# RWKV-style attention with a feed-forward chain: its small products on column halves, the first bonuses summed on TensorE, k and v without padding, and a new order of block 0

## The chip, the cores and the metric

The kernel runs on one NeuronCore of a Trainium2 chip. Its time is the device time of one execution in microseconds (us), as a median of three runs. A core has TensorE (PE, matrix products into PSUM), VectorE (DVE), ScalarE (ACT), GpSimd (POOL, which can't read PSUM) and SyncE (SP), which here only issues DMAs. ACT issues some DMAs at the start too. Each engine works through its own instructions in order; semaphores join them.

## The reference

A linear attention with decay, over 4 batches, 8 heads, 768 steps and 48 channels a head, and behind it two feed-forward parts on the 3072 tokens:

```python
for t in range(S):                       # state: (B, H, 48, 48)
    cur = u * k[t] (outer) v[t]
    y[t] = r[t] @ (state + cur)
    state = w * state + k[t] (outer) v[t]
x = y as (B*S, 384)
h = x @ w_in                             # 384 -> 2048
x = (max(h, 0) + alpha * min(h, 0)) @ w_out
h = ((x @ w1) * (x @ w2)) @ w3           # 384 -> 1024 -> 1024
return h @ w_out2                        # 1024 -> 384
```

The weights come as 64-bit floats.

## The kernel before

**Tiling.** The 768 steps are cut in 6 blocks of 128. In each block the 8 heads are taken as 4 pairs; a pair in a block, with all 4 batches, is a unit (24 units, n = 0 to 23; the pairs are taken in the order 3, 0, 1, 2, so units 0 to 3 are pairs 3, 0, 1, 2 of block 0). The two heads of a pair lie in partitions 0 to 47 and 64 to 111 where channels are on partitions.

**A unit's steps** have short names that the order of the work is written in. `ld` loads r and k with channels on partitions (`rk`) and r, k, v with steps on partitions (`nat`; in the loads of units 0 to 3 these parts are called r, k, a, b, v, with the unit's number). `rs` and `ks` (L178, L184) scale r and k by powers of w (`pw`), `S` (L239) multiplies them to 128x128 scores, `q` (L194) and `red` (L206) make the bonus u·r·k of each step as a sum over channels, `am` (L213) puts it on a diagonal, `fill` (L250) copies the scores in beside it under a mask. `kk` (L228) scales k for the state, `U` (L255) makes the state's update as a product of it with v, `car` (L270) adds it to the state. `Y` (L285) makes the output: the state product (state with `rs`, in blocks 1 to 5 only) and, into the same PSUM tile, the value products (v with `am`). The value products write each head on its own column half of TensorE's array (outputs from PSUM partition 0 or 64); the update and the state product use up to 112 columns at once. `ph` and `pl` (L333, L338) split y into a high and a low part for the feed-forward part, and `mv` (L326, L306) moves the rows of pair 3 by DMA into free partitions of the others' tile `x`: unit 0's into chunk 2, unit 1's into chunk 0, unit 2's into chunk 1.

**The feed-forward part** takes three products for each (high by high, low by high, high by low). In a block it has 16 features f: `P` (L475) is the first product (9 matmuls over the three chunks of `x`), `r` and `s` the activation (ACT, then DVE at L493), `hl` splits the result (ACT, then POOL), `D` (L512) the second product (9 matmuls into `acc`).

**The weights of the first part** are made in block 0 from 64-bit words: `is` or `issue` loads a raw tile (SP), `cA` (L117, ACT) widens it, `cd` (L122, three DVE instructions, with the PSUM bank `uy` as scratch) assembles the 32-bit value, `cB` (ACT) rounds it to the high part, `cl` (L138) makes the low part, on DVE for the features in WIV and WOV and on POOL for the others. There are 32 such tiles: w_in of feature 0, then by turns w_in of f+1 and w_out of f (`cdi11` would be w_in of feature 11).

**Order.** Everything is scheduled by hand. Block 0 and the preparation of block 1 run by the list STARTUP (L49): each word is a step, issued to its engines in that order. LOADS (L64) is the order of the first loads; words with a star go over ACT's queue, the others over SP's. The lists in L46 and L47 say which engine takes which unit's step: RV and KV the units whose `rs` and `ks` are on DVE (else POOL), AMA those whose `am` is on ACT (else DVE), CARA those of block 0 whose `car` is on ACT. Blocks 1 to 4 repeat the pattern MIDDLE (L37), block 5 has LAST; in blocks 1 to 4 a unit's `U` and `Y` follow each other on TensorE.

**Ahead of TensorE's first work** it multiplies zeros (`warm`, L740): WARM = 6 products of 128x512.

Of the kernel before, what the change touches and what calls it, by code (L numbers as in the profile page):

```python
# [17 lines left out]
P = 128  # L18
C = 128
# [9 lines left out]
R = 64 + D  # L29
VW = 2 * 64  # L30
ZERO = 64
WARM = 6
LEAD = 1
# [11 lines left out]
ORDER = (3, 0, 1, 2)  # L45
RV, KV, AMA, CARA = (1, 2), (0, 1, 2, 4, 5, 6), (0, 1, 2, 3, 5, 7), (2, 3, 6, 7)  # L46
WIV, WOV = (3,), (0, 4, 5, 7, 10, 11, 14, 15)  # L47
PIN = 16
STARTUP = """  # L49
ld4 q0 rs0 pw0 ks0 S0 red0 ks1 rs1 am0 S1 fill0 ks2 rs2 q1 kk0 U0 q2 red1 am1 Y0 red2 fill1 S2 q3 ph0 cA issue1  # L50
red3 Y1 rs3 issue1 am2 pl0 mv0 ks3 car0 cd ph1 am3 S3 fill2 Y2 ld5 fill3 ph2 cB kk1 pl1 pl2 mv1 Y3 cA U1 cd ks4
mv2 cB cA cA q4 red4 cl issue1 car1 kk3 cl cd cB cd ph3 cl issue1 issue1 issue1 rs4 cB pl3 U3 mv3 P0 cA am4 q5
r0 P1 is cA cl cd s0 r1 kk4 cd S4 kk2 hl0 P2 cB cl U2 fill4 car3 cB cl cA r2 s1 hl1 cA Y4 cd U4 cB car2 P3
issue1 cd cA cl cB s2 r3 D0 cd ks5 cA rs5 issue1 ld6 cl is cB s3 P4 ph4 is is cl D1 hl3 is hl2 cA cd issue1 cB
r4 is is red5 car4 pl4 cd s4 am5 cB cl cA hl4 cl D2 cA cd mv4 P5 S5 is cB kk5 cl cd r5 is s5 cB cA cl cA cd
fill5 hl5 ld7 cB P6 r6 cl cA cd cB D3 s6 rs6 cl cd U5 hl6 ks6 P7 r7 cB s7 cA cl cA cd cd Y5 cB is kk6 cl D4 is
ph5 cA car5 cB q6 cl hl7 P8 D5 r8 red6 is cd P9 is s8 S6 cB pl5 cA cd cl hl8 r9 cB is cl D6 q7 is am6 cA cd cA
s9 cB is cl hl9 cd P10 is cB cl cA r10 fill6 cA cd cB ks7 s10 cA cl cd hl10 D7 cd rs7 P11 is r11 s11 cB cl Y6
kk7 ph6 cB hl11 U6 cl cA mv5 cA D8 cd cB is is cd P12 r12 cB s12 D9 cl cA cl pl6 car6 cA cd hl12 cB P13 cd r13
cl D10 cd cl s13 cA S7 ld8 cd cB cl mv6 hl13 is cA red7 cB P14 cl q8 am7 cd fill7 r14 cA cA cB cd is D11 P15 ks8  # L60
cA U7 s14 cd Y7 kk8 rs8 cB r15 cd is ph7 D12 cl is D13 s15 cB cl cA car7 hl15 cl is red8 pl7 hl14 mv7 is cB am8
ld9
"""
LOADS = """  # L64
b1 r0* a0 k3 keep* a1* a2 b0 v0 k1 r1* v3 v2 brief* k0* a3* k2* r2 b2 v1 r3 b3
"""
# [4 lines left out]
def tile_kernel(ctx: ExitStack, tc: tile.TileContext, a: dict, out: bass.AP):  # L71
# [18 lines left out]

    w_sb = const.tile([R, NHP], F32, name="w_sb")
    keep = const.tile([P, P + DM + M1], F32, name="keep")
# [5 lines left out]
    w128 = const.tile([R, NHP, 1], F32, name="w128")  # L98
    w2 = const.tile([P, NHP, R], F32, name="w2")
    state = const.tile([R, NHP, B, R], F32, name="state")  # L100
# [48 lines left out]
    def load(n, now=True):  # L149
        i, hp = UNITS[n]  # L150
        cuts = [0, B * 2 * D, B * (2 * D + R), B * (2 * D + R + VW)]
        src = [a["rkT"][i, hp, :, m] for m in range(2)]
        src += [a["nat"][i, hp, :, lo:hi] for lo, hi in zip(cuts, cuts[1:])]
        if n in (2, 3):
            w = "wi" if n == 2 else "wo"
            t = [spare(f"{w}{11 + m}", list(x.shape), f"in{m}") for m, x in enumerate(src)]
        else:
            rk = ld.tile([R, 2, B, C], F32, tag="rk", name="rk")
            nat = ld.tile([P, cuts[-1]], F32, tag="nat", name="nat")
            t = [rk[:, 0], rk[:, 1]] + [nat[:, lo:hi] for lo, hi in zip(cuts, cuts[1:])]  # L160
            if now:
                nc.sync.dma_start(out=rk, in_=a["rkT"][i, hp])
                nc.sync.dma_start(out=nat, in_=a["nat"][i, hp])
        if not now:
            fetch.update({f"{x}{n}": (t[m], src[m]) for m, x in enumerate("rkabv")})
        un[n] = dict(
            rk=t[0:2],
            r=t[2].rearrange("p (b j d) -> p b j d", b=B, j=2),
            k=t[3].rearrange("p (b d) -> p b d", b=B),
            v=t[4].rearrange("p (b d) -> p b d", b=B),  # L170
        )
# [22 lines left out]
    def prep_q(n):  # L194
        i, hp = UNITS[n]
        t = un[n]
        q1 = work(n, [P, B, 2, D], "q1", "wi8")
        t["q1"] = q1
        nc.gpsimd.tensor_tensor(
            out=q1, in0=t["r"], in1=bc(u_sb[:, hp], B).rearrange("p b (j d) -> p b j d", j=2), op=ALU.mult  # L200
        )
        k = t["k"]
        heads = bass.AP(k.tensor, k.offset, [list(k.ap[0]), [R, B], [64, 2], [1, D]])
        nc.gpsimd.tensor_tensor(out=q1, in0=q1, in1=heads, op=ALU.mult)

# [22 lines left out]
    def prep_k2(n):  # L228
        i, hp = UNITS[n]
        t = un[n]  # L230
        if i < NB - 1:
            if 0 < n < NHP:
                k2 = spare("wi9" if n == 2 else "wo8", [P, B, R], "k2")
            else:
                k2 = wk.tile([P, B, R], F32, tag="k2", name="k2")
            nc.gpsimd.tensor_tensor(out=k2, in0=t["k"], in1=bc(w2[:, hp], B), op=ALU.mult)
# [18 lines left out]
    def update(n):  # L255
# [4 lines left out]
        pool, tag = (ps_a, f"acc{2 * (n % 2)}") if n < NHP else (ps_s, "s")  # L260
        pu = pool.tile([R, B, 2, D], F32, tag=tag, name="pu")
        for b in range(B):
            nc.tensor.matmul(
                out=pu[:, b],
                lhsT=t["k2"][:, b], rhs=t["v"][:, b].rearrange("p (j d) -> p j d", j=2)[:, :, 0:D],
                start=True, stop=True,
            )
        t["pu"] = pu

    def carry(n):  # L270
# [4 lines left out]
        for j in range(2):  # L275
            s = state[64 * j:64 * j + D, hp, :, 64 * j:64 * j + D]
            if i == 0:
                (nc.scalar.copy if n in CARA else nc.vector.tensor_copy)(out=s, in_=pu[64 * j:64 * j + D, :, j])
                continue
            nc.vector.scalar_tensor_tensor(  # L280
                out=s, in0=s, scalar=w128[64 * j:64 * j + D, hp],
                in1=pu[64 * j:64 * j + D, :, j], op0=ALU.mult, op1=ALU.add,
            )

    def out_y(n):  # L285
        i, hp = UNITS[n]
# [412 lines left out]
    def transposes(_):  # L699
        pw2 = ps_u.tile([P, NHP, P], F32, tag="uy", name="pw2")  # L700
        for hp in range(NHP):
            nc.tensor.transpose(
                out=pw2[:, hp, 0:R], in_=up[:, hp, ZERO - 1:ZERO - 1 + C], identity=ident[0:R, 0:R]
            )
        nc.scalar.copy(out=w2, in_=pw2[:, :, 0:R])

    with tc.manual_schedule():
        todo += first_weights()
        nc.sync.dma_start(out=w_sb, in_=a["w"])
        junk = wk.tile([P, N], F32, tag="am", name="junk", bufs=2)  # L710
        nc.vector.memset(junk, 0.0)
# [134 lines left out]
def layout(x):  # L846
# [20 lines left out]
    rn = toks(r).reshape(NB, NHP, C, B * 2 * D)  # L867
    kn = np.zeros((NB, NHP, C, B, 2, 64), k.dtype)
    kn[..., :D] = toks(k)
    kn = kn.reshape(NB, NHP, C, B, P)[..., :R].reshape(NB, NHP, C, B * R)  # L870
    vn = np.zeros((NB, NHP, C, B, VW), v.dtype)
    vn[..., 0:D] = toks(v)[..., 0, :]
    vn[..., 64:R] = toks(v)[..., 1, :]
    o["nat"] = np.ascontiguousarray(np.concatenate([rn, kn, vn.reshape(NB, NHP, C, B * VW)], axis=3))
# [57 lines left out]
```

## Time and profile before

| | us |
|---|---|
| median of 3 runs | 861.36 |
| lowest and highest | 859.84, 861.59 |
| the profiled execution | 858.42 |
| its span, first to last instruction | 856.6 |
| TensorE busy in it | 831.0 |
| POOL, DVE, ACT busy | 388.2, 387.0, 347.3 |

TensorE's records of 32-bit products come in two per product; "x16" stands for 8 products. Busy times of matmuls overlap, so the time that one takes in a sequence is read from its start to the next one's start. In a row of a timeline stand the start and the duration in us, engine, line, operation, output<-inputs, shape and count, and in brackets the idle time before it with what ended it. Rows of the page and the trace stand below, in groups.

### The profile page before, as it was taken

Reading aid. Unit: us, or ns where it says so; the run is one execution under the profiler, and the core shown is the slowest. Engines: PE = TensorE matmul, PEld = TensorE weight load, DVE = VectorE, ACT = ScalarE, POOL = GpSimd, SP = SyncE. Lnnn points to the kernel's source line nnn. Section 1 sums busy time; section 2 is a strip of 40 time slices with the busy share of each in tenths; the row PEclk is TensorE's granted clock in tenths of the full one; section 3 lists DMA queues with packets and bytes.
Section 4 is the critical chain, followed back from the end, with each engine's and each line's share of the span. In section 5 each row is a group of like instructions: output and inputs, shape, how many; then the busy total and the mean of one; then the engine's idle time right before and its main releaser. Section 6 shows DMA issues by size and latency. Waiting matters only on the chain.

```text
span 856.6 us, 11700 instructions
## 1 busy us (share of the span) xinstructions
PE 831.0 (97%) x4320; PEld 686.5 (80%) x4320; DVE 387.0 (45%) x611; ACT 347.3 (41%) x689; POOL 388.2 (45%) x327
## 2 busy tenths in 40 slices
PE   7599999999999999999999999999999999999997
PEld 4487788888888888888888888888888888888885
DVE  6889997987697777763332211111110101010100
ACT  3576675555555554544334442221222222222121
POOL 5676875666577658664432252121141322323211
PEclk8899999999999999999999999999999999999999
DMA  9656565776777776733223550432100202020001
GB/s 280 200 191 195 150 198 176 233 241 214 227 226 194 207 214 203 209 113 102 83 78 115 197 186 19 135 135 99 44 31 0 75 1 74 0 74 1 1 37 42
DMA packets 45445, 111.37 MB, mean 130 GB/s; under 512 B 5249, under 2 KB 12546, under 8 KB 45378
## 3 DMA queue, kind: packets, MB, share of 16 engines
q1 hardware_dynamic: 44290, 108.81, 40.7%
q10 hardware_dynamic: 1088, 1.71, 0.7%
q8 instruction: 36, 0.59, 0.3%
q14 instruction: 31, 0.25, 0.1%
HBM read 80.88 MB, written 27.26 MB: 126 GB/s over the span
## 4 chain that ended last, share of the span: by engine, by line
PE 89%; DVE 5%; DMA 2%; issue 2%; ACT 1%; SPq 0%; POOL 0%; DVEq 0%; ACTq 0%
PE acc L114 11%; PE acc L113 11%; PE acc L115 11%; PE ph L113 8%; PE ph L114 7%; PE ph L115 7%; PE pb L114 4%; PE pa L114 4%; PE pa L115 4%; PE pb L115 4%; PE pb L113 4%; PE pa L113 4%; PE sc L246 2%; PE py L299 2%; PE py L292 2%
## 5 line engine op out<-in xcount | busy, mean ns | idle before, releaser
L110 POOL TENSOR_TENSOR gl<-g,gh 128x512 fp32r<-128x512 f32 x96 | 125.4, 1307 | 173.2 <-ACT gh L109 168.8
L110 POOL TENSOR_TENSOR gl<-p,gh 128x512 fp32r<-128x512 f32 x48 | 62.1, 1293 | 238.2 <-ACT gh L109 238.2
L770 DVE TENSOR_TENSOR p<-p,pb 128x512 f32<-128x512 f32 x48 | 33.0, 688 | 249.9 <-PE pb L115 249.9
L113 PE MATMUL ph<-x,wi 128*128 128x512 f32 x288 | 117.2, 407 | 3.9 <-DMA x<-e 3.4
L493 DVE SCALAR_TENSOR_TENSOR g<-g,keep,p 128x512 f32<-128x512 f32 x80 | 71.8, 897 | 105.2 <-ACT p L488 95.1
L114 PE MATMUL ph<-x,wi 128*128 128x512 f32 x288 | 113.9, 395 | 2.7 <-POOL wi L139 2.7
L115 PE MATMUL ph<-x,wi 128*128 128x512 f32 x288 | 113.2, 393 | 0.0
L113 PE MATMUL acc<-gh,wo 128*128 128x512 f32 x288 | 112.5, 391 | 0.0
L115 PE MATMUL acc<-gl,wo 128*128 128x512 f32 x288 | 112.3, 390 | 0.0
L114 PE MATMUL acc<-gh,wo 128*128 128x512 f32 x288 | 112.1, 389 | 0.0
L765 ACT COPY p<-pa 128x512 f32<-128x512 f32 x48 | 28.2, 587 | 200.6 <-PE pa L115 200.6
L487 ACT ACTIVATE g<-ph 128x512 f32<-128x512 f32 x96 | 57.2, 596 | 88.4 <-PE ph L115 83.6
L109 ACT CAST gh<-g 128x512 fp32r<-128x512 f32 x96 | 59.3, 619 | 67.2 <-DVE g L493 66.5
L113 PEld LDWEIGHTS ph<-x,wi 128*128 128x128 f32 x288 | 54.6, 189 | 19.6 <-ACT wi L136 4.3
L114 PEld LDWEIGHTS ph<-x,wi 128*128 128x128 f32 x288 | 54.6, 190 | 15.1 <-POOL wi L139 4.8
L115 PEld LDWEIGHTS ph<-x,wi 128*128 128x128 f32 x288 | 54.5, 189 | 11.5
L115 PEld LDWEIGHTS acc<-gl,wo 128*128 128x128 f32 x288 | 54.1, 188 | 11.6 <-POOL gl L110 0.4
L113 PEld LDWEIGHTS acc<-gh,wo 128*128 128x128 f32 x288 | 54.1, 188 | 11.6 <-issue 0.3
L114 PEld LDWEIGHTS acc<-gh,wo 128*128 128x128 f32 x288 | 54.1, 188 | 11.1
L115 PE MATMUL acc<-gl,m 128*128 128x512 f32 x144 | 56.2, 390 | 0.0
L114 PE MATMUL acc<-gh,m 128*128 128x512 f32 x144 | 56.1, 390 | 0.0
L113 PE MATMUL pa<-x,w 128*128 128x512 f32 x144 | 56.0, 389 | 0.0
(106 smaller groups left out, 1617.0 us busy)
## 6 DMA issues: line engine op xcount, KB each, us to landing
nat<-in_nat SPq DMA_DIRECT2D x20, 672.0 KB, 6.7
raw<-in_wA SPq DMA_DIRECT2D x32, 384.0 KB, 3.6
s<-raw SPq DMA_DIRECT2D x32, 384.0 KB, 3.5
rk<-in_rkT SPq DMA_DIRECT2D x20, 448.0 KB, 6.4
raw<-in_wB SPq DMA_DIRECT2D x16, 384.0 KB, 4.4
raw<-in_w3T SPq DMA_DIRECT2D x16, 384.0 KB, 4.6
w<-s SPq DMA_DIRECT2D x16, 384.0 KB, 3.1
x2d<-o SPq DMA_DIRECT2D x18, 256.0 KB, 2.4
```

The source lines that it names most:

```text
L109: nc.scalar.copy(out=dst_h, in_=src)
L110: (lo or nc.gpsimd).tensor_tensor(out=dst_l, in0=src, in1=dst_h.bitcast(F32), op=ALU.subtract)
L113: nc.tensor.matmul(out=o, lhsT=wh, rhs=xh, start=first, stop=False)
L114: nc.tensor.matmul(out=o, lhsT=wl, rhs=xh, start=False, stop=False)
L115: nc.tensor.matmul(out=o, lhsT=wh, rhs=xl, start=False, stop=last)
L246: nc.tensor.matmul(out=sc[j][:, b], lhsT=t["ks"][o:o + D, b], rhs=t["rs"][o:o + D, b], start=True, stop=True)
L292: nc.tensor.matmul(out=py[:, b], lhsT=state[:, hp, b], rhs=t["rs"][:, b], start=b == 0, stop=False, skip_group_check=True,)
L299: nc.tensor.matmul(out=py[o:e, b], lhsT=t["v"][:, b, o:e], rhs=t["am"][:, B * j + b], start=i == 0 and b == 0, stop=True, skip_group_check ...
L487: nc.scalar.activation(out=g, in_=ph, func=ACTF.Relu, scale=-1.0)
L493: nc.vector.scalar_tensor_tensor(out=g, in0=g, scalar=alpha[:, f:f + 1], in1=p, op0=ALU.mult, op1=ALU.add)
L765: nc.scalar.copy(out=g, in_=pa)
L770: nc.vector.tensor_tensor(out=g, in0=g, in1=pb, op=ALU.mult)
```

## The change

- k and v lie in DRAM and in the tiles without padding: 384 columns each, where k had 448 and v 512.
- Update (L255): two products per batch, one a head, each with 48 weight columns and 48 streamed columns, on the column half of its head; before, one product of 112 weight columns and 96 streamed ones. k2 has 384 columns in place of 448.
- State product (L285): two products per batch, of 64 and 48 weight columns, on the two column halves; before, one of 112.
- Value products: as before, with v's new offsets.
- Bonus of units 0 to 2 (QPE): `q` is one DVE instruction on the tiles with channels on partitions (u times k times r), `red` four products on TensorE with a two-column tile of ones (`heads`), into PSUM bank `uy`, and a copy on ACT. The `a` loads of these units are left out, and w comes together with u (`wu`).
- RV, KV, AMA, CARA, WIV and WOV have new members. `ks` of units 1, 2, 4, 5, 6 goes from DVE to POOL, `rs` of unit 0 from POOL to DVE, `am` of unit 2 from ACT to DVE, `car` of unit 1 from DVE to ACT; five low halves of weights are on DVE in place of nine.
- STARTUP and LOADS have new orders. ACT issues five of the first loads, not eight.
- Ahead of TensorE's first work stand 14 products of zeros of 128x256.

```diff
-WARM = 6
+WARM = 14
-RV, KV, AMA, CARA = (1, 2), (0, 1, 2, 4, 5, 6), (0, 1, 2, 3, 5, 7), (2, 3, 6, 7)
-WIV, WOV = (3,), (0, 4, 5, 7, 10, 11, 14, 15)
+RV, KV, AMA, CARA = (0, 1, 2), (0,), (0, 1, 3, 5, 7), (1, 2, 3, 5)
+WIV, WOV = (3, 5, 15), (11, 14)
+MVA = 0
+QPE = (0, 1, 2)
 STARTUP = """
-ld4 q0 rs0 pw0 ks0 S0 red0 ks1 rs1 am0 S1 fill0 ks2 rs2 q1 kk0 U0 q2 red1 am1 Y0 red2 fill1 S2 q3 ph0 cA issue1
-red3 Y1 rs3 issue1 am2 pl0 mv0 ks3 car0 cd ph1 am3 S3 fill2 Y2 ld5 fill3 ph2 cB kk1 pl1 pl2 mv1 Y3 cA U1 cd ks4
-mv2 cB cA cA q4 red4 cl issue1 car1 kk3 cl cd cB cd ph3 cl issue1 issue1 issue1 rs4 cB pl3 U3 mv3 P0 cA am4 q5
...
+ks1 ks3 pw0 ks0 rs0 ld4 S0 kk0 q0 red0 rs1 am0 rs2 U0 q1 S1 red1 q2 am1 fill0 Y0 q3 fill1 Y1 rs3 S3 car0 cA ph0
+cA red3 pl0 cd ks2 issue1 red2 S2 kk1 am2 fill2 mv0 rs4 q4 ph1 am3 Y2 U1 ph2 fill3 cB red4 ks4 cd pl1 cA cd pl2
+issue1 ld5 mv1 cB issue1 mv2 issue1 cA Y3 car1 cl cB kk3 cl cd ph3 pl3 S4 mv3 U3 cB P0 cl cA q5 r0 cd cl is cB
+cA am4 P1 r1 kk2 cl is s0 cd hl0 s1 car3 cB cA is U2 fill4 cl P2 kk4 hl1 is cA r2 cd cB rs5 U4 issue1 cl P3 is
+Y4 car2 cd cA is ld6 cB r3 s2 issue1 cd issue1 cl D0 s3 cA cB P4 ph4 issue1 cl is D1 issue1 hl3 hl2 cA cd car4
+cB kk5 r4 red5 ks5 D2 am5 cd cl s4 cB cA pl4 cl hl4 cd P5 cA cB D3 is is cl S5 ld7 cd P6 r5 cA s5 cB cl hl5 cA
...
 LOADS = """
-b1 r0* a0 k3 keep* a1* a2 b0 v0 k1 r1* v3 v2 brief* k0* a3* k2* r2 b2 v1 r3 b3
+brief k3 a1 b3* b1 k2 a0 r0 r1 keep b0* v0* a3 v2 a2 r2 k1* r3 b2 v3 v1 k0*
...
     def prep_q(n):
+        if n in QPE:
+            t["q1"] = q1 = work(n, [R, B, C], "q1", "wi8")
+            nc.vector.scalar_tensor_tensor(
+                out=q1, in0=t["rk"][1], scalar=wu[:, 1, hp:hp + 1], in1=t["rk"][0][:, :, ::-1],
+                op0=ALU.mult, op1=ALU.mult,
+            )
+            return
...
     def bonus(n):
+        if n in QPE:
+            pq = ps_u.tile([P, B * 2], F32, tag="uy", name="pq")
+            for b in range(B):
+                nc.tensor.matmul(
+                    out=pq.rearrange("p (j b) -> p b j", j=2)[:, b], lhsT=t["q1"][:, b], rhs=heads, start=True, stop=True
+                )
+            nc.scalar.copy(out=t["q"], in_=pq)
+            return
...
     def update(n):
-        pu = pool.tile([R, B, 2, D], F32, tag=tag, name="pu")
+        pu = pool.tile([R, B, D], F32, tag=tag, name="pu")
         for b in range(B):
-            nc.tensor.matmul(
-                out=pu[:, b],
-                lhsT=t["k2"][:, b], rhs=t["v"][:, b].rearrange("p (j d) -> p j d", j=2)[:, :, 0:D],
-                start=True, stop=True,
-            )
+            for j in range(2):
+                h = slice(D * j, D * j + D)
+                nc.tensor.matmul(
+                    out=pu[64 * j:64 * j + D, b], lhsT=t["k2"][:, b, h], rhs=t["v"][:, b, h], start=True, stop=True
+                )
...
     def out_y(n):
+        sides = [(64 * j, min(64 * j + 64, R)) for j in range(2)]
         if i > 0:
             for b in range(B):
-                nc.tensor.matmul(
-                    out=py[:, b], lhsT=state[:, hp, b], rhs=t["rs"][:, b], start=b == 0, stop=False,
-                    skip_group_check=True,
-                )
+                for o, e in sides:
+                    nc.tensor.matmul(
+                        out=py[o:e, b], lhsT=state[:, hp, b, o:e], rhs=t["rs"][:, b],
+                        start=b == 0, stop=False, skip_group_check=True,
+                    )
...
-        warm = ps_h.tile([P, N], F32, tag="h", name="warm")
-        for _ in range(WARM):
-            nc.tensor.matmul(out=warm, lhsT=junk[:, 0:P], rhs=junk, start=True, stop=True)
+        def busy(k):
+            held = any(("U", n) in fin and ("car", n) not in fin for n in (0, 2))
+            idle = ps_a.tile([P, 2 * P], F32, tag="acc2" if held else "acc0", name="idle")
+            for _ in range(k):
+                nc.tensor.matmul(out=idle, lhsT=zeros[:, 0:P], rhs=zeros, start=True, stop=True)
...
+        busy(WARM)
```

## Rows read from the trace of the kernel before

**Rows 1.** The page's busy time of each engine (us, share of span, instructions).
```profile
PE 831.0 (97%) x4320; PEld 686.5 (80%) x4320; DVE 387.0 (45%) x611; ACT 347.3 (41%) x689; POOL 388.2 (45%) x327
```

**Rows 2.** Who waited for whom, TensorE, 40 to 125 us: total, times, longest.
```profile
PE ph L113 <- DMA x<-e: 3.4, 1, 3.4
PE ph L114 <- POOL wi L139: 2.7, 4, 1.0
PE ph L113 <- ACT wi L136: 0.6, 1, 0.6
```

**Rows 3.** Busy us in the window: PE, PEld, DVE, ACT, POOL, then clock, DMA.
```profile
80.00:100.00 20.00, 18.35 (x90) 14.00 (x90) 18.59 (x34) 12.50 (x25) 15.48 (x15) 1.00 0.61 192
```

**Rows 4.** Timeline of the start: start, duration, engine, line, what, idle before.
```profile
3.39 0.34 ACTq L719 DMA_DIRECT2D brief<-in_brief  x1
...
11.03 0.81 DVE L188 TENSOR_TENSOR ks<-rk,pw 112x512 f32<-112x512 f32 x1 [3.31 <-ACT pw L732]
...
14.39 1.48 DVE L182 TENSOR_TENSOR rs<-rk,pw 112x512 f32<-112x512 f32 x1
...
19.67 1.87 PE L299 MATMUL py<-am,nat 128*64 128x128 f32 x16
...
35.49 2.55 SPq L308 DMA_DIRECT2D x<-e  x4
...
41.13 0.77 PE L113 MATMUL ph<-x,wi 128*128 128x512 f32 x1 [3.36 <-DMA x<-e]
...
42.08 1.69 DVE L220 TENSOR_TENSOR am<-keep,q 128x1024 f32<-128x1024 f32 x1
```

**Rows 5.** Timeline of TensorE: update, state, value products of a unit in block 1.
```profile
196.54 0.93 PE L263 MATMUL pu<-nat,k 128*112 128x96 f32 x8
197.31 1.05 PE L292 MATMUL py<-rs,state 112*112 112x128 f32 x8
198.29 1.09 PE L299 MATMUL py<-am,nat 128*64 128x128 f32 x16
199.31 0.50 PE L113 MATMUL ph<-x,wi 128*128 128x512 f32 x1
199.65 0.39 PE L114 MATMUL ph<-x,wi 128*128 128x512 f32 x1
```

**Rows 6.** Chain of waits and timeline, TensorE in block 0: records at both clocks, S4.
```profile
42.33 0.43 PE ph L115
...
45.79 0.23 PE ph L115
...
47.33 1.16 PE L246 MATMUL sc<-rs,ks 48*128 48x128 f32 x16
48.42 0.50 PE L113 MATMUL ph<-x,wi 128*128 128x512 f32 x1
```

**Rows 7.** Groups by form, weight loads, 180 to 380 us: busy us, mean ns.
```profile
L263 PEld LDWEIGHTS pu<-nat,k 128*112 128x112 f32 x72 | 8.4, 177 | 0.8
...
L299 PEld LDWEIGHTS py<-am,nat 128*48 128x48 f32 x72 | 7.4, 122 | 0.0
```

**Rows 8.** DMA issues to 45 us (KB, us to landing); the same for tile x.
```profile
brief<-in_brief ACTq DMA_DIRECT2D x1, 128.0 KB, 5.3
...
DMA to landing us min/median/max: 4.2/4.7/5.2
```

**Rows 9.** Groups by form, VectorE, 0 to 125 us: busy us, mean ns, idle before.
```profile
L128 DVE SCALAR_TENSOR_TENSOR bits<-raw,bits 128x384 uint32<-128x384 uint32 x32 | 18.0, 562 | 1.1
...
L253 DVE COPY_PREDICATED am<-mask,sc 128x512 f32<-128x512 uint8 x16 | 11.2, 731 | 4.1 <-ACT am L218 3.9
L139 DVE TENSOR_TENSOR wo<-t,wo 128x384 fp32r<-128x384 f32 x7 | 4.6, 661 | 0.0
...
L188 DVE TENSOR_TENSOR ks<-rk,pw 112x512 f32<-112x512 f32 x5 | 4.2, 841 | 4.6 <-ACT pw L732 3.3 <-DMA rk<-in_rkT 1.3
...
L340 DVE TENSOR_TENSOR x<-py,x 112x512 fp32r<-112x512 f32 x4 | 2.6, 681 | 0.0
```

More of the change, by code (lines that the diff above doesn't have):

```diff
@@ L29 @@
 R = 64 + D
-VW = 2 * 64
 ZERO = 64
-WARM = 6
+WARM = 14
 LEAD = 1
@@ L52 @@
-mv2 cB cA cA q4 red4 cl issue1 car1 kk3 cl cd cB cd ph3 cl issue1 issue1 issue1 rs4 cB pl3 U3 mv3 P0 cA am4 q5
[L53 to L61, printed above, removed]
@@ L62 @@
-ld9
+ks1 ks3 pw0 ks0 rs0 ld4 S0 kk0 q0 red0 rs1 am0 rs2 U0 q1 S1 red1 q2 am1 fill0 Y0 q3 fill1 Y1 rs3 S3 car0 cA ph0
[3 more added lines that the diff above has]
+Y4 car2 cd cA is ld6 cB r3 s2 issue1 cd issue1 cl D0 s3 cA cB P4 ph4 issue1 cl is D1 issue1 hl3 hl2 cA cd car4
@@ new lines @@
+cB kk5 r4 red5 ks5 D2 am5 cd cl s4 cB cA pl4 cl hl4 cd P5 cA cB D3 is is cl S5 ld7 cd P6 r5 cA s5 cB cl hl5 cA
+mv4 cd fill5 cd cB r6 U5 cl rs6 cB Y5 is cA s6 ks6 is cl hl6 cd cA cd P7 cB D4 r7 cl cA cB s7 q6 cl car5 ph5 cd
+kk6 red6 cA cB is D5 cl is is hl7 P8 r8 cd cB s8 P9 S6 pl5 cl cA is cd am6 hl8 r9 is cA cB cl D6 mv5 cA cd D7 s9
+cB ks7 cl is hl9 cd cB cl cA fill6 P10 r10 cd P11 is cB s10 q7 cl cA hl10 cA cd cd U6 D8 r11 cB cl cd s11 cB cA
+hl11 cl cB Y6 cd rs7 cA is ph6 cB P12 cl r12 cd is pl6 cB mv6 cA cl D9 cA P13 kk7 s12 car6 hl12 cd cB cd ld8 r13
@@ L63 @@
+cA cB D10 cl S7 s13 cl cd q8 red7 P14 hl13 cB is cl cA am7 cB cA cd cB fill7 is cl D11 P15 cd cd is cl U7 rs8 is
+cd Y7 ks8 ld9 r15 D12 cA s15 cA r14 s14 is cl car7 red8 kk8 ph7 D13 pl7 cB am8 hl15 cl mv7 is hl14 cA
 """
 LOADS = """
-b1 r0* a0 k3 keep* a1* a2 b0 v0 k1 r1* v3 v2 brief* k0* a3* k2* r2 b2 v1 r3 b3
+brief k3 a1 b3* b1 k2 a0 r0 r1 keep b0* v0* a3 v2 a2 r2 k1* r3 b2 v3 v1 k0*
 """
@@ L89, in bc @@
         return ap.unsqueeze(1).to_broadcast([ap.shape[0], n, ap.shape[1]])
-    w_sb = const.tile([R, NHP], F32, name="w_sb")
+    wu = const.tile([R, 2, NHP], F32, name="wu")
+    w_sb = wu[:, 0]
+    heads = const.tile([R, 2], F32, name="heads")
     keep = const.tile([P, P + DM + M1], F32, name="keep")
@@ L98, in tile_kernel @@
     w128 = const.tile([R, NHP, 1], F32, name="w128")
-    w2 = const.tile([P, NHP, R], F32, name="w2")
+    w2 = const.tile([P, NHP, 2 * D], F32, name="w2")
+    zeros = const.tile([P, 2 * P], F32, name="zeros")
     state = const.tile([R, NHP, B, R], F32, name="state")
@@ L150, in load @@
         i, hp = UNITS[n]
-        cuts = [0, B * 2 * D, B * (2 * D + R), B * (2 * D + R + VW)]
+        cuts = [0, DM, 2 * DM, 3 * DM]
         src = [a["rkT"][i, hp, :, m] for m in range(2)]
@@ L155, in load @@
             w = "wi" if n == 2 else "wo"
-            t = [spare(f"{w}{11 + m}", list(x.shape), f"in{m}") for m, x in enumerate(src)]
+            t = [None if m == 2 and n in QPE else spare(f"{w}{11 + m}", list(x.shape), f"in{m}") for m, x in enumerate(src)]
         else:
@@ L167, in load @@
             rk=t[0:2],
-            r=t[2].rearrange("p (b j d) -> p b j d", b=B, j=2),
+            r=t[2] and t[2].rearrange("p (b j d) -> p b j d", b=B, j=2),
             k=t[3].rearrange("p (b d) -> p b d", b=B),
@@ L201, in prep_q @@
         )
-        k = t["k"]
-        heads = bass.AP(k.tensor, k.offset, [list(k.ap[0]), [R, B], [64, 2], [1, D]])
-        nc.gpsimd.tensor_tensor(out=q1, in0=q1, in1=heads, op=ALU.mult)
+        nc.gpsimd.tensor_tensor(
+            out=q1, in0=q1, in1=t["k"].rearrange("p b (j d) -> p b j d", j=2), op=ALU.mult
+        )
     def bonus(n):
@@ L232, in prep_k2 @@
             if 0 < n < NHP:
-                k2 = spare("wi9" if n == 2 else "wo8", [P, B, R], "k2")
+                k2 = spare("wi9" if n == 2 else "wo8", [P, B, 2 * D], "k2")
             else:
-                k2 = wk.tile([P, B, R], F32, tag="k2", name="k2")
+                k2 = wk.tile([P, B, 2 * D], F32, tag="k2", name="k2")
             nc.gpsimd.tensor_tensor(out=k2, in0=t["k"], in1=bc(w2[:, hp], B), op=ALU.mult)
@@ L277, in carry @@
             if i == 0:
-                (nc.scalar.copy if n in CARA else nc.vector.tensor_copy)(out=s, in_=pu[64 * j:64 * j + D, :, j])
+                (nc.scalar.copy if n in CARA else nc.vector.tensor_copy)(out=s, in_=pu[64 * j:64 * j + D])
                 continue
@@ L281, in carry @@
                 out=s, in0=s, scalar=w128[64 * j:64 * j + D, hp],
-                in1=pu[64 * j:64 * j + D, :, j], op0=ALU.mult, op1=ALU.add,
+                in1=pu[64 * j:64 * j + D], op0=ALU.mult, op1=ALU.add,
             )
@@ L289, in out_y @@
         t["py"] = py = pool.tile([R, B, C], F32, tag=tag, name="py")
+        sides = [(64 * j, min(64 * j + 64, R)) for j in range(2)]
         if i > 0:
             for b in range(B):
-                nc.tensor.matmul(
-                    out=py[:, b], lhsT=state[:, hp, b], rhs=t["rs"][:, b], start=b == 0, stop=False,
-                    skip_group_check=True,
-                )
-        for b in range(B):
-            for j in range(2):
-                o, e = 64 * j, min(64 * j + 64, R)
-                nc.tensor.matmul(
-                    out=py[o:e, b], lhsT=t["v"][:, b, o:e], rhs=t["am"][:, B * j + b],
+                for o, e in sides:
+                    nc.tensor.matmul(
+                        out=py[o:e, b], lhsT=state[:, hp, b, o:e], rhs=t["rs"][:, b],
+                        start=b == 0, stop=False, skip_group_check=True,
+                    )
+        for b in range(B):
+            for j, (o, e) in enumerate(sides):
+                nc.tensor.matmul(
+                    out=py[o:e, b], lhsT=t["v"][:, b, D * j:D * j + e - o], rhs=t["am"][:, B * j + b],
                     start=i == 0 and b == 0, stop=True, skip_group_check=True,
@@ L307, in move_e @@
         for j in range(2):
-            nc.sync.dma_start(
+            (nc.scalar if i < MVA else nc.sync).dma_start(
                 out=xt[i][64 * j + D:64 * j + 64, :, c].bitcast(F32),
@@ L704, in transposes @@
             )
-        nc.scalar.copy(out=w2, in_=pw2[:, :, 0:R])
+        nc.scalar.copy(
+            out=w2.rearrange("p g (j d) -> p g j d", j=2),
+            in_=pw2.rearrange("p g (j d) -> p g j d", j=2)[:, :, :, 0:D],
+        )
     with tc.manual_schedule():
         todo += first_weights()
-        nc.sync.dma_start(out=w_sb, in_=a["w"])
-        junk = wk.tile([P, N], F32, tag="am", name="junk", bufs=2)
-        nc.vector.memset(junk, 0.0)
+        nc.sync.dma_start(out=wu, in_=a["wu"])
+        nc.vector.memset(heads, 0.0)
+        for j in range(2):
+            nc.vector.memset(heads[64 * j:min(64 * j + 64, R), j:j + 1], 1.0)
+        nc.vector.memset(zeros, 0.0)
         brief = cv.tile([P, 2 * P], F32, tag="t", name="brief")
@@ L717, in tile_kernel @@
         for x in LOADS.split():
+            if x[0] == "a" and int(x.rstrip("*")[1:]) in QPE:
+                continue
             k = x.rstrip("*")
@@ L806, in tile_kernel @@
         table["xx"] = extra
+        table["wm"] = busy
+        busy(WARM)
         per_unit = "q rs ks red am S fill Y kk U car ph pl mv ld".split()
@@ L867, in layout @@
     rn = toks(r).reshape(NB, NHP, C, B * 2 * D)
[L868 to L874, printed above, removed]
+    kn, vn = (toks(t).reshape(NB, NHP, C, B * 2 * D) for t in (k, v))
+    o["nat"] = np.ascontiguousarray(np.concatenate([rn, kn, vn], axis=3))
     wp = np.ones((NHP, 2, 64), w.dtype)
     wp[:, :, :D] = w.reshape(NHP, 2, D)
-    o["w"] = np.ascontiguousarray(wp.reshape(NHP, P)[:, :R].T)
     o["wrow"] = np.ascontiguousarray(w.reshape(1, DM))
```

## Prediction, made before the result

> **What bounds the kernel now.** I read the page's busy line first: TensorE is busy 831.0 of 856.6 us [rows 1], so the end is TensorE's own work plus the time in which it waits or runs slowly. The list of TensorE's waits between 40 and 125 us comes next: apart from the start of the first feed-forward product (3.4 us, for a DMA into `x`) there are only five, four of them for POOL's low halves of `wi` (2.7 us) and one for ACT's high half (0.6), 3.3 us in all [rows 2]. The list goes to 125 us and shows no other. The windows view says who is behind those waits: in 80 to 100 us VectorE is busy 18.59 of 20 us, TensorE 18.35 [rows 3]. So the time is made of three parts: when P0 starts (41.13 us, [rows 4]), how far VectorE's weight assembly lags after that, and the dense stretch to the end, where only what TensorE executes counts. DMA, POOL, ACT and VectorE have slack in that last part, so the shorter k and v, the 384-column k2 and the smaller `nat` loads of blocks 1 to 5 are worth nothing there.
>
> **The dense stretch: update and state on column halves.** In one unit [rows 5] the update takes 0.77 us from its start to the state product's, the state product 0.98, the value products 1.02, and the step from the first `ph` matmul to the second 0.34 where 0.23 is usual [rows 6]. So leaving the column halves costs 0.11; I take the same for entering them, which today falls between state and value products and makes the state product itself 0.98 - 0.11 = 0.87 for 8 records, 0.109 each. The 16 value records stream the same 128 columns in 0.064 each: two halves do run at the same time, at half of 0.109 plus about 0.009.
> After the change the entry comes ahead of the update and all three run on halves. State product: the form of the value products, 16 records, 1.02. Update: 16 records with 48 weight columns and 48 streamed columns, a form that no row shows. From below: streaming alone, two at once, 0.109 x 48/128 / 2 = 0.020, plus the 0.009, is 0.029 a record, 0.47 us. From above: the value record's 0.064, which is 1.02 us. Between them: today's update record lasts 0.77/8 = 0.096 although its 96 columns stream in 0.109 x 96/128 = 0.082, so its 112-column weight load sets it; the load rows say that loads get shorter with fewer columns (177 ns for 112, 122 for 48) [rows 7]. Loads taken in turn at 0.096 x 48/112 = 0.041 make 0.66, with the 0.009 a record 0.80. I take the middle of these two, 0.73.
> Per unit: 0.11 + 0.73 + 1.02 against 0.77 + 0.98, +0.11 us. Sixteen units (blocks 1 to 4) have update and state product: +1.8. The four units of the last block have no update: 0.11 + 1.02 - 0.98 = +0.15 each, +0.6. Sum **+2.4 us** (bounds: -1.8 at 0.47, +7.0 at 1.02). Block 0 has no state product, and its updates stand in TensorE's idle time but for one.
>
> **The start: when P0 can begin.** P0 needs the moved rows `x<-e` of chunk 0 (mv1, issued by SP) and three matmuls later those of chunk 1 (mv2). I walk VectorE's new order. The start loads carry 960 KB less by their shapes (4 x 96 KB of padding of k and v, three `a` loads of 192 KB), and k0, now ACT's fifth load as `brief` was, is issued at 3.39 like it; `brief`, 128 KB, took 5.3 us to land [rows 8]; k0 has 224 KB, so I put it at about 9.2 and ks0 starts 1.8 us earlier than today's 11.03 [rows 4]. It takes 0.84. Then come six two-input operations on 112x512 (rs0, q0, rs1, rs2, q1, q2), where today VectorE had four of that kind in the same place and POOL made q. Such an operation took 0.84 as a mean of five, and 1.48 while POOL was at work [rows 4, 9]; POOL is at work all that time (ks1, ks3, kk0, q3, rs3, ks2), so I take 1.4: 8.4, done at about 18.4. This is the largest price on this path (bounds 5.0 to 8.9). The two fills of units 0 and 1 are 4 x 0.73 = 2.9, then car0, red3 and pl0, which I take at pl's 0.68 each, and one weight assembly, 3 x 0.56 = 1.67: 25.0. am2, now VectorE's (am4 took 1.69), must wait for red2, which on TensorE is queued behind Y0, Y1 and S3 and needs the PSUM bank `uy` that the assembly has just used; behind it S2, Y2 and U1 wait. Those start at 19.7 after fill0 and take about 1.9 each if the clock has dropped as it had today (Y0 1.87, [rows 4]): red2 at 25.5. Four products of two columns are not in the trace; between nothing and an update's 0.8 I take 0.5, and 0.2 for ACT's copy: am2 starts at 26.2, 1.2 us idle. am2, fill2, fill3, red4, one assembly, pl1: 33.7. One more assembly and pl2: 36.1. SP issues a move in about 0.64 (four in 2.55), and it lands 4.2 to 5.2 us later [rows 4, 8]: chunk 0 at about 39.7, chunk 1 at 41.5. P0's three chunks last 1.3 us each at the low clock (three times 0.43, [rows 6]), so P0 runs without a stop from 40.2: **-0.9 us** (bounds -3.6, if VectorE's six take 0.84 and Y0 to S3 run at the high clock for part of the way, and +1.9, if red2's turn and the moves come late). That is little for so many moved words: VectorE starts earlier but does more ahead of pl2, while today SP was the late one.
> S4 stood behind P0 and P1; now it stands before P0, where TensorE waits anyway: 1.09 us, the distance from its start to the next `ph` matmul in the dense part [rows 6]: **-1.1 us**. If P0 came at once behind S4 this would be nothing.
> P0 itself starts at the lower of the two clock levels (a 512-column record 0.43 us, later 0.23, [rows 6]), as TensorE has waited 3.4 us before. The same wait stays, so I give nothing for it. The 14 zero products of 256 columns in place of 6 of 512 have a sixth more columns: nothing, since S0 behind them waits for rs0, to about 11.5 in the walk above, and even a later S0 is covered until fill0 at 18.4.
>
> **The start: the weight assembly.** From P0 to the assembly of the last `wi` that TensorE waits for (wi11), VectorE's order had 18 assemblies, 10 slopes, 4 low halves, 2 am, 2 fills, 2 ks, 2 red, 2 carries, 2 pl. The new order has the same but no ks (2 x 0.84) and 2 low halves (2 x 0.66 less) [rows 9]: 1.7 + 1.3 = 3.0 us less. The ks and the low halves go to POOL, which idled there. TensorE's needs come 0.9 + 1.1 = 2.0 us earlier. VectorE's start of this stretch comes earlier too: today am4 at 42.1 [rows 4], then the assembly behind pl3 (36.1, an assembly and two pl: 39.1), 3.0 us. So the assembly gains 6.0 on its old time and TensorE's need 2.0: of the 3.3 us of waits [rows 2] nothing should be left; as the last wait stays close, I count **-2.8 us** (bounds 0 and -3.3).
> Sum of the start: -0.9 - 1.1 - 2.8 = **-4.8 us**.
>
> **Sum.** +2.4 - 4.8 = -2.4. The profiled execution took 858.42 us, 1.8 around its span; it would be 856.0. The median of the runs is 861.36, 2.9 above the profiled one, and I carry the difference over: **859.0 us**.
>
> **Rivals.**
> *Halves overlap fully.* Weight loads of one half run beside the other's matmuls, the update costs 0.47: -1.8 - 4.8 = -6.6, 854.8 us. For it: the value records show two halves streaming at once [rows 5]. Against: no row shows loads of two halves at once, and the full-width update was held by its load. The Trainium skill, "TensorEngine Tiling (Array Packing)", Tiling Modes, Key Properties, says that different tiles execute weight loads and matmuls in parallel; by that rule it comes out so.
> *Slower: records have a floor.* If TensorE can't start records faster than the value products do, whatever their size, the update becomes 16 x 0.064 = 1.02 and the dense stretch pays +7.0: 861.36 + 7.0 - 4.8 = 863.6 us. It decides from 0.88 us an update, 55 ns a record, where 16 x (0.88 - 0.62) + 0.6 eats the 4.8. For it: no row here is faster than 0.064 a record. Against: those records have 128 columns to stream, which by itself makes 0.055. The Trainium skill, "TensorE: Matmul & The Clock Gate", Part 1, "Wait — 56ns, not 53.3ns?", has an instruction path on which each matmul costs about 62 ns and small matmuls are bound by it; by that the update would be 0.99. No run here shows which path is in use.
> *The start doesn't come earlier.* VectorE's front load (q0 to q2, rs0, am2) makes P0 late at 43.0: +1.9 - 1.1 - 2.8 + 2.4 = +0.4, 861.8 us. For it: two more operations of the costly kind ahead of the fills; against: k0 arrives earlier.
> *The start comes much earlier.* VectorE's six are quick, P0 starts near 37.9 and so soon behind U3 that the clock stays high: a further -2.3 and -2.1 (ten records at 0.43 instead of 0.23, [rows 6]), 854.6 us.
>
> **From these to the numbers.** Forecast 0.36 (own range 857.0 to 861.0, the bounds of update and P0 together), full overlap 0.16, floor 0.20, no earlier start 0.18, much earlier 0.10. Faster by over 0.2% means below 859.6, and 0.2% is about what can be told from no change here: three quarters of the forecast's chance (0.27), 0.16 and 0.10: 0.53. Slower, above 863.1: the floor and a part of the late start, 0.23. The rest, 0.24, is within 0.2%. The range 854.3 to 864.0 takes in both outer cases.
>
> **What would show it.** Right: in a steady unit update start to state start about 0.73, state to value 1.02, value to `ph` 1.02, and about 0.11 of delay ahead of the update; P0 near 40; TensorE's waits for `wi` gone; S4 ahead of P0. Wrong: an update near 1.0 or near 0.5; a P0 behind 42 with VectorE at q1 or q2 past 19 us; waits for POOL's `wi` still there (then POOL, with ks and more low halves, has become what VectorE was).

## The result and the profile after

The changed kernel took 853.36 us (median of six, 852.88 to 854.10), the kernel before in the same runs 860.65: a ratio of 0.9917 (95% interval 0.9902 to 0.9931), 6 to 8 us faster. The forecast was 859.0 with a range from 854.3; the time lies below the range.

The page of the changed kernel, as in [rows 1]:

```profile
span 851.1 us, 12398 instructions
...
PE 831.7 (98%) x4680; PEld 686.9 (81%) x4680; DVE 386.2 (45%) x605; ACT 345.9 (41%) x686; POOL 387.4 (46%) x329
```

The span is 5.5 us shorter than before's 856.6, and TensorE's busy time is the same, though it has 360 records more: a sum of busy times can't say where the 5.5 us come from, since records on two halves overlap. The place is found by a mark that both kernels pass after the same work: S7, the scores of unit 7 (the tail of block 0). The chain of waits, first before, then after (start, duration, what):

```profile
112.80 1.09 PE sc L246 x16
```
```profile
112.78 1.09 PE sc L264 x16
```

Both reach it at the same time. All of the 5.5 us lie behind it, in the dense stretch: 856.6 - 112.80 = 743.8 us against 851.1 - 112.78 = 738.3. In this pair of executions the new start gave nothing in sum; how much the start before varies is told below. One unit of the dense stretch, timeline of TensorE, as [rows 5]:

```profile
194.58 0.56 PE L283 MATMUL pu<-nat,k 128*48 128x48 f32 x16
194.98 1.05 PE L312 MATMUL py<-rs,state 112*64 112x128 f32 x16
195.86 1.05 PE L318 MATMUL py<-am,nat 128*48 128x128 f32 x16
196.83 0.50 PE L116 MATMUL ph<-x,wi 128*128 128x512 f32 x1
197.17 0.40 PE L117 MATMUL ph<-x,wi 128*128 128x512 f32 x1
```

From start to start the update takes 0.40 us (0.77 before, 0.73 forecast), the state product 0.88 (0.98; 1.02), the value products 0.97 (1.02). The scores of units that follow each other stand 20.14 us apart in the chain (189.25 and 209.39); before it was 20.55.

The start of the changed kernel: ACT's loads, the waits of VectorE and ACT, then TensorE up to P0 (timeline, as [rows 4]).

```profile
2.92 3.93 ACTq L745 DMA_DIRECT2D rk<-in_rkT  x2
...
12.55 0.69 DVE L191 TENSOR_TENSOR ks<-rk,pw 112x512 f32<-112x512 f32 x1 [5.29 <-DMA rk<-in_rkT]
...
13.12 0.22 ACT L764 ACTIVATE keep<-keep 128x16 f32<-128x16 f32 x1 [3.38 <-DMA keep<-in_keep]
...
13.90 2.08 PE L264 MATMUL sc<-rs,ks 48*128 48x128 f32 x16 [3.64 <-DVE rs L185]
15.91 1.86 PE L222 MATMUL pq<-heads,q 112*128 112x2 f32 x8
17.70 0.89 PE L283 MATMUL pu<-nat,k 128*48 128x48 f32 x16
18.52 2.08 PE L264 MATMUL sc<-rs,ks 48*128 48x128 f32 x16
20.53 1.86 PE L222 MATMUL pq<-heads,q 112*128 112x2 f32 x8
22.32 1.97 PE L318 MATMUL py<-am,nat 128*64 128x128 f32 x16
...
44.38 0.80 PE L116 MATMUL ph<-x,wi 128*128 128x512 f32 x1
```

k0, ACT's last load, is issued near 6.5 us, where ACT's issuing stood still, and ks0 waits for it until 12.55. Then TensorE runs S0, red0, U0, S1, red1 without a gap from 13.90 to 22.32, at half the clock (granted 0.50 from 14 to 26 us), and Y0 stands behind them. P0 starts at 44.38, 3.25 us later than in the profiled execution of the kernel before.

### The profile page after: what moved, and what is told of

Read it like the earlier page. It is cut to its first block, busy times and chain, and to the rows that moved or that the text cites. A ratio compares the mean times of both kernels' runs of the same rounds, so it can differ in the third digit from the quotient of the medians.

```text
span 851.1 us, 12398 instructions
## 1 busy us (share of the span) xinstructions
PE 831.7 (98%) x4680; PEld 686.9 (81%) x4680; DVE 386.2 (45%) x605; ACT 345.9 (41%) x686; POOL 387.4 (46%) x329
## 4 chain that ended last, share of the span: by engine, by line
PE 91%; DVE 3%; POOL 2%; ACT 1%; DMA 1%; issue 1%; SPq 0%; DVEq 0%; POOLq 0%; ACTq 0%
PE acc L116 11%; PE acc L118 11%; PE acc L117 11%; PE ph L116 8%; PE ph L117 7%; PE ph L118 7%; PE pb L118 4%; PE pa L118 4%; PE pb L117 4%; PE pa L117 4%; PE pa L116 4%; PE pb L116 4%; PE sc L264 3%; PE py L318 2%; PE py L312 2%; PE pf L118 1%
## 5 line engine op out<-in xcount | busy, mean ns | idle before, releaser
L512 DVE SCALAR_TENSOR_TENSOR g<-g,keep,p 128x512 f32<-128x512 f32 x80 | 76.6, 957 | 102.5 <-ACT p L507 89.4
```

The source lines that it names most:

```text
L512: nc.vector.scalar_tensor_tensor(out=g, in0=g, scalar=alpha[:, f:f + 1], in1=p, op0=ALU.mult, op1=ALU.add)
```

## Experiments

"Before" is the kernel before, timed on the same chip in the same rounds; each ratio is to it, with its 95% interval.

**Both halves, nothing else.** In the kernel before (k and v still padded):

```diff
-            nc.tensor.matmul(out=pu[:, b], lhsT=t["k2"][:, b], rhs=<v of both heads>, ...)
+            for j in range(2):
+                h = slice(64 * j, 64 * j + D)
+                nc.tensor.matmul(out=pu[64*j:64*j+D, b], lhsT=t["k2"][:, b, h], rhs=t["v"][:, b, h], ...)
...
-                nc.tensor.matmul(out=py[:, b], lhsT=state[:, hp, b], rhs=t["rs"][:, b], ...)
+                for o, e in ((0, 64), (64, R)):
+                    nc.tensor.matmul(out=py[o:e, b], lhsT=state[:, hp, b, o:e], rhs=t["rs"][:, b], ...)
```

> The kernel before with update and state product on column halves; padding, orders and start as before. Theory A (the gain is the dense stretch alone, a unit's period 20.14 instead of 20.55 us, and the new start nets nothing): 16 units x 0.41 = -6.6 us in the span, time ratio about 0.992, as the whole change. Theory B (part of the gain is the new start or the shorter k and v): -3 to -5 us, and the whole change is faster than this kernel by over 1.5 us.

854.06 us, 0.9930 (0.9908 to 0.9951), and a unit's period of 20.13: theory A. The few lines above are the change's whole gain as far as it can be measured. New start, shorter k and v, the products for the bonuses and the new engines for single steps make 0.0013 together, about 1.1 us, and the intervals of the two kernels overlap. The profiled execution, with the start as before, passes S7 late:

```profile
115.89 1.09 PE sc L246 x16
```

From there to its end at 854.2 us it takes 738.3 us, as the changed kernel does. So the dense stretch has all of its gain from the column halves, and the start of before varies by some 3 us between executions (112.80 and 115.89).

**Each half alone.** The first of the two hunks, then the second.

> The kernel before with only the update on column halves, the state product full width. Theory A1 (the update's short records make the gain: 0.77 to about 0.40 us; the state product costs nothing either way): the update takes 0.40, but the column halves are then entered and left twice in a unit, 0.1 us each time, so the unit's period falls by 0.2 to 0.3, span -3 to -5 us. Theory A2 (switching costs nothing, only the update counts): period -0.37, span -6 us.

> The kernel before with only the state product on column halves, the update full width. Theory A1 (each entry into the column halves costs about 0.1 us, and the state product on halves itself is no longer than full width): period as before, 20.5 us, the entry only moves ahead of the state product; time the same within 1 us. Theory A3 (halves are shorter for the state product in any company): period 20.3 or less, -3 to -5 us.

Update alone: 857.24, 0.9960 (0.9944 to 0.9976). State product alone: 860.29, 0.9994 (0.9982 to 1.0005), no change. The chain of waits shows why; its pieces end where the next begin, so they add up. Before, then update alone, state alone, and the changed kernel:

```profile
196.70 0.77 PE pu L263 x8
197.47 0.89 PE py L292 x8
198.36 1.02 PE py L299 x15
```
```profile
196.49 0.49 PE pu L265 x16
196.98 1.06 PE py L292 x8
198.04 1.02 PE py L299 x15
```
```profile
199.33 0.77 PE pu L263 x8
200.10 1.02 PE py L293 x15
201.12 0.88 PE py L300 x16
```
```profile
194.65 0.49 PE pu L283 x16
195.15 0.88 PE py L312 x15
196.03 0.88 PE py L318 x16
```

Sixteen records of 128 columns on halves take 0.88, and 1.02 where they are the first behind a full-width product: 0.14 for entering. A full-width product behind halves pays too: the state product 1.06 instead of 0.89. The sums are 2.68, 2.57, 2.67 and 2.25. So the update's halves save 0.28 in the chain, of which a full-width state product behind it eats 0.17; with the state product on halves as well, which by itself is no shorter (0.88 for 0.89), the group enters once. Theory A1 held in kind for both, but the gain of the update alone was smaller than I had put it: the period is 20.43, 0.12 less and not 0.2 to 0.3, and the update takes 0.49 to the next start, not 0.40, with a full-width product behind it.

**What an update record lasts by.** Here each update record streams v of both heads, 96 columns, of which half is thrown away; the weights stay at 48 columns.

```diff
-        pu = pool.tile([R, B, D], ...)
+        pu = pool.tile([R, B, 2 * D], ...)
...
-                    out=pu[64 * j:64 * j + D, b], ..., rhs=t["v"][:, b, h], ...
+                    out=pu[64 * j:64 * j + D, b], ..., rhs=t["v"][:, b], ...
```

> The changed kernel with update records that stream 96 columns (v of both heads, the half that isn't needed is not read) at the same 48 weight columns. Theory S (an update record lasts as long as half its columns' streaming, two halves at once, or a small floor): the update grows from 0.40 to about 16 x 0.041 = 0.66 us, the unit's period from 20.14 to 20.40, span about +4 us. Theory W (the weight loads, one after the other, set it, as the prediction had it): it stays at 0.40, time the same.

858.75 us, 0.9971 (0.9954 to 0.9988), which loses over half of the gain again; theory S. Its chain:

```profile
198.33 0.80 PE pu L283 x16
199.12 0.88 PE py L312 x16
```

From start to start in the timeline the update takes 0.70 us. With 48, 96 and 128 streamed columns a record costs 25, 44 and 55 ns: by columns, about 0.38 ns for each more. The weight loads (48 columns in the update, 64 and 48 by turns in the other products) don't show. Whether the 25 ns are also the least that a record can take, no run tells.

**Bonuses back on POOL and VectorE**, in the changed kernel:

```diff
-QPE = (0, 1, 2)
+QPE = ()
```

> The changed kernel with the bonuses of units 0 to 2 back on POOL and VectorE (and their three loads back), all else as changed. Theory C (the bonus products on TensorE, 1.86 us each at the low clock and in the way of U0, S1 and Y0, made P0 late, 44.4 us): P0 comes earlier than 44.4 by 1 to 3 us and the time falls by as much or by a part of it. Theory D (the late k0, landing at 12.5, and the order hold P0; POOL's two passes a unit and 576 KB more of loads cost more than the products): P0 at 45 or later, time the same or up to 3 us longer.

852.22 us, 0.9902 (0.9884 to 0.9920), no difference from the changed kernel that can be told. The first records of P0's chain come later (S0 at 17.78, held by rs0, which takes 3.64 us on VectorE there and 0.69 in the changed kernel) and P0 about 0.7 us earlier. Neither theory as told: as I read it, what the products cost in TensorE's order, POOL's passes cost in VectorE's. Tried again below with other loads.

**Zeros up to S0**, in the changed kernel:

```diff
-ks1 ks3 pw0 ks0 rs0 ld4 S0 ...
+ks1 ks3 pw0 wm9 ks0 rs0 ld4 S0 ...
```

> The changed kernel with 9 more products of zeros behind the transposes, so that TensorE works from 10.3 to about 14.1 us, where it waited 3.6 us before S0. Theory E (the drop to the low clock at S0 made the products of the start long, and they lie on the way to P0): S0 takes 1.1 instead of 2.0, the bonus products 1.0 instead of 1.8, P0 at 41 to 42 instead of 44.4, time -2 to -3 us. Theory F (VectorE, ACT and the loads hold the start, TensorE's clock matters little): P0 within 1 us of 44.4, time the same within 1 us.

850.02 us, 0.9877 (0.9858 to 0.9897), about 3 us faster than the changed kernel: theory E. Timeline of TensorE:

```profile
13.93 1.16 PE L264 MATMUL sc<-rs,ks 48*128 48x128 f32 x16 [0.22 <-DVE rs L185]
15.43 1.02 PE L222 MATMUL pq<-heads,q 112*128 112x2 f32 x8 [0.34 <-DVE q L202]
...
19.36 3.10 PE L318 MATMUL py<-am,nat 128*64 128x128 f32 x18
```

S0 starts as late as in the changed kernel, but Y0 is on at 19.36 instead of 22.32, since S0 takes 1.1 and red0 0.95 us. P0 starts at 42.33 instead of 44.38: the low clock at S0 made about 2 us of P0's delay.

**The order of the loads.** k0 as ACT's first load; then all first loads in the order of need, three of them on ACT, and ks3 behind kk0; the changed kernel beside them.

```diff
-brief k3 a1 b3* b1 k2 a0 r0 r1 keep b0* v0* a3 v2 a2 r2 k1* r3 b2 v3 v1 k0*
+brief k3 k0* b1 b3* k2 r0 r1 keep b0* v0* a3 v2 r2 k1* r3 b2 v3 v1
```
```diff
-brief k3 a1 b3* b1 k2 a0 r0 r1 keep b0* v0* a3 v2 a2 r2 k1* r3 b2 v3 v1 k0*
+brief k0 r0* keep k1* r1 b0* k2 r2 v0 k3 b1 b3 a3 r3 v1 v2 b2 v3
```

> The changed kernel with k0 as the first of ACT's loads instead of the last, all else as changed. Theory G (k0, landing at 12.5 us, holds VectorE's whole chain and so P0): ks0 starts by 9 us, S0 by 11 instead of 13.9, P0 2 to 3 us earlier, time -2 to -3 us. Theory H (behind k0 the next late load, keep at 13.1, or TensorE's low clock holds the chain): S0 earlier but am0 not before 17, P0 within 1 us of 44.4, time within 1 us.

> The changed kernel with the first loads in the order in which the first steps need them (k0, r0, keep, k1, r1, b0 first; three loads on ACT instead of five) and ks3 behind kk0. Theory G: keep lands by 8, S0 at about 9.5, am0 by 12, P0 at 40 or earlier, time -4 us or more against the changed kernel. Theory H: the low clock and later loads (k2, r2, k3, b3) keep P0 at 42 or later, time -2 us at most.

> The changed kernel itself, timed beside the others on one chip: 0.990 to 0.993 of before, P0 at 44 to 45. It has no rival; it is the measure for the two kernels with other loads.

851.09 us, 0.9901 (0.9885 to 0.9918); 848.01, 0.9857 (0.9841 to 0.9874); and the changed kernel 853.01, 0.9917. With k0 first S0 starts at 12.74 and P0 at 42.77: a part of theory G, as the next late loads (r0, keep) then hold the chain; the time can't be told from the changed kernel's. With all in order:

```profile
8.21 0.63 DVE L191 TENSOR_TENSOR ks<-rk,pw 112x512 f32<-112x512 f32 x1
```
```profile
9.71 1.16 PE L264 MATMUL sc<-rs,ks 48*128 48x128 f32 x16
...
35.85 0.80 PE L116 MATMUL ph<-x,wi 128*128 128x512 f32 x1
```

P0 starts 8.5 us earlier than in the changed kernel, the median falls by 5.0: theory G. All of it lies in the start: S7 comes at 104.58, and from there to the end it takes 738.2 us, as the changed kernel does. The run doesn't separate the order from what came with it: S0 follows the zeros without a wait and runs at the high clock (1.16 us), which by itself gave 3 us above; ACT issues three loads and not five; and ks3 has another place.

**On these loads: the bonuses back, and more zeros.** The first adds a0, a1, a2 to the loads and sets QPE = (); the second adds `wm1` behind red1 and `wm2` behind S2 and ahead of Y3.

> The changed kernel with the loads in the order of need, timed once more beside its two variants: 844 to 849 us, P0 at about 36. It has no rival; it is the measure for the variants.

> The kernel with the loads in the order of need and the bonuses of units 0 to 2 back on POOL and VectorE (three loads more). Theory C (the bonus products on TensorE are in the way): -1 to -3 us against the same loads with the products. Theory D (POOL's two passes a unit and 576 KB more cost more, once the loads are in order): P0 2 us or more later than 36 and the time +1 to +3 us.

> The kernel with the loads in the order of need and five products of zeros in three places where TensorE waits (behind red1, behind S2, ahead of Y3). Theory E (the low clock still stretches the products up to P0 and P0 itself): Y0 to S3 and P0's first records at the high clock, -1 to -3 us. Theory F (VectorE and ACT hold the chain now, and zeros in the queue delay what is behind them): the same or up to +2 us.

848.24 us, 0.9859 (0.9836 to 0.9881); with the bonuses back 850.75, 0.9887 (0.9868 to 0.9907); with more zeros 847.13, 0.9835 (0.9809 to 0.9860). The bonus products on TensorE are worth about 2.5 us once the loads come in order (theory D; the intervals overlap a little, but every execution with them was faster than every one without): without them S1 starts at 17.55, as rs1 stands behind the bonus steps, with them at 13.47. The zeros decide nothing: P0 starts at 37.94 with them and at 36.77 without, and the intervals overlap. Loads in the order of need, with or without these zeros, beat both given kernels.

## Why the prediction was wrong

**The dense stretch failed, in sign: +2.4 forecast, about -6.6 found** (sixteen units by 20.55 - 20.14 = 0.41, thirteen of them behind S7; in the last block, without updates, 19.80 became 19.78). The step was "Loads taken in turn at 0.096 x 48/112 = 0.041 make 0.66, with the 0.009 a record 0.80. I take the middle". An update record costs 0.025, not 0.046. The run with 96 columns shows that its streamed columns set it. The loads of the two halves don't wait for each other as I had them do: 0.025 is less than the 0.041 that I had put on one load. The load rows agree, 16 loads of 124 ns each within 0.44 us (group of weight loads, as [rows 7], then timeline).

```profile
L283 PEld LDWEIGHTS pu<-nat,k 128*48 128x48 f32 x144 | 4.0, 124 | 3.2 <-issue 2.1 <-DVE bits L131 0.7 <-DVE t L134 0.4
```
```profile
194.58 0.44 PEld L283 LDWEIGHTS pu<-nat,k 128*48 128x48 f32 x16 [0.35 <-issue]
```

I had taken it that a 112-column load holds up the update of the kernel before, which no run tested, and had carried that over to a form in which the load is hidden. Of the rival "Halves overlap fully" the mechanism was right; I gave it 0.16. The Trainium skill, "TensorEngine Tiling (Array Packing)", Tiling Modes, Key Properties, had the rule for it (loads and matmuls of different tiles in parallel), and the runs with this update on halves agree, at 25 ns a record. That the rival's 854.8 us came near the time is luck: its dense stretch (-1.8 us) was 5 us too slow and its start (-4.8) 5 us too fast. The floor rival is refuted by the same 25 ns.

The same step counted the entry twice. The 0.064 a value record, from which the 0.009 "over" the streaming came, held the entry into the halves: 16 records take 0.88 without and 1.02 with it. I put 1.02 for state and value product each and 0.11 for the entry besides. In the chain the three take 0.49 with the entry, 0.88 and 0.88, together 2.25 for 2.68. Even the bound "from below" of -1.8 us was 5 us too high, mostly for this reason.

**The start failed too: -4.8 forecast, nothing found up to S7.** The two errors have opposite signs, so the forecast of the span, 2.4 us shorter for 5.5, looks better than its parts were.

**P0: 40.2 forecast, 44.4 found.** Three terms of the walk failed. k0 was to land at 9.2 since ACT's fifth load before was issued at 3.39; here ACT issued k1 at 2.92 and then nothing until k0 at 6.53, and ks0 could start only at 12.55. In the chain of waits k0's issue follows the landing of k3 (6.51): as I read it, a load is issued when an earlier one has made room. The "largest price", six operations of VectorE at 1.4, was too high: five took 0.68 to 0.75 and one 1.56, 5.1 us in all. These two cancel, by luck: VectorE was done with them at 18.56, where the walk had 18.4. What is left is the third: the bonus products were to take 0.5 each, and I had only red2 in the walk. They take 1.8 at the low clock, and ACT's am1, for which the fill of unit 1 waits, stands behind red1. The chain of waits from there to am2:

```profile
20.59 1.81 PE pq L222 x8
...
22.63 2.46 ACT am L236 x8
25.10 0.74 DVE am L271
25.89 1.94 PE py L318 x14
27.83 1.94 PE sc L264 x16
29.78 1.00 PE pq L222 x8
...
31.05 1.88 DVE am L238
```

am2 was forecast for 26.2 and started at 31.05. The moves of chunks 0 and 1 landed after 2.3 to 4.2 us and not 4.2 to 5.2, which gave a part back.

**S4 ahead of P0: it ran there** (at 40.3 to 43.6, while P0's inputs were made). Whether it was free, as forecast, isn't shown: S4 at the low clock and U3 lie directly ahead of P0, which starts without a wait.

**The weight assembly: right for VectorE's work, not for its start, and so not for the sum.** Waits of TensorE from 40 us on, as [rows 2], after:

```profile
PE pu L283 <- POOL k L254: 1.3, 1, 1.3
PE ph L117 <- POOL wi L142: 1.2, 2, 0.6
...
PE pu L283 <- DVE am L271: 0.4, 1, 0.4
```

The waits for `wi` fell from 3.3 to 1.2, but 1.3 are new: U4 waits for kk4, which now stands on POOL behind the low part of the first feature (hl0) and stood ahead of it before. So 0.4 us of the 2.8 came. VectorE began this stretch at 44.85 us (42.08 before, 39.1 forecast). The last wait for `wi`, in P11 in both kernels, ends here in the chain, first before, then after:

```profile
97.57 0.50 PE ph L114
```
```profile
97.37 0.50 PE ph L117
```

So the stretch did get 3.0 us shorter, as counted, but its late start ate this, and TensorE gained 0.2. So P0's delay by itself, as I read it, didn't cost its 3.25 us: with an earlier P0 alone TensorE would have waited for `wi` longer. The same sum from TensorE's side: P0 +3.25; five records at the low level and not ten, -1.0; S4 no longer behind P0, -1.1; waits -0.4; the shorter updates and outputs up to unit 6 about -0.5, an estimate from the distances of their starts. That is nearly nothing, as S7 shows.

**The 2.9 us** by which the median stood over the profiled run were carried over, and shouldn't have been: the kernel before ran from 858.9 to 862.2, the changed one from 852.9 to 854.1. The medians differ by 7.3, the spans of the profiled runs by 5.5. The profiled execution before had a quick start: the kernels with the update alone, the state product alone and both on halves, all with before's order of the start, have P0 at 41.74, 44.14 and 42.35, and their granted clock from 20 to 30 us was 0.67, 0.50 and 0.67 against 0.76. What makes it vary was not tried. So the new start may be worth about 1 us against a usual start of before, which these runs can't tell from nothing.

## What to carry to other kernels

Where small products already run on column halves, put their neighbours there too, as a group: price a record by its streamed columns, two at a time, and pay for entering and leaving once for each group. A price read from a neighbour in the trace must be cleared of what that neighbour pays for its place in the order. And a start bound by loads is won by issuing them in the order of need: this, with the higher clock that came with it, gave 5 us, where a new order of all steps had given about 1 us, if anything.

## What the runs showed that was not expected

The clock fell while TensorE had work. With zeros up to S0 it was busy without a gap worth naming from 10 to 22 us, yet the granted clock went to the lower level (windows: busy us of TensorE, clock, DMA):

```profile
14.00:18.00 4.00, 3.66 (x57) 1.00 1.05 321
18.00:22.00 4.00, 4.00 (x27) 0.55 0.61 176
```

What it ran before the fall were scores of 48 rows, bonus products of 2 columns and an update of 48 columns. Which of these, if any, let it fall is open.

DMA issues held a computing engine up: ACT reached its first computing instruction at 6.88 us in the changed kernel, behind five loads, at 8.85 in the kernel before, behind eight, and at 2.16 in the one with three. The number isn't all: with k0 as the first of five it was 4.97.
